# Loads of the head spread over three issuers, query in 1 KB runs, and the combined matrix M built through VectorE turns of w2

## The chip, the core and the metric

One core of a Trainium2 chip runs the whole program. The metric is the device time of one execution in microseconds. TensorE is called PE, VectorE DVE, ScalarE ACT, GpSimd POOL, SyncE SP; PEld is PE's load of stationary operands, and SPq is SP issuing DMAs.

## What is computed

Three layers follow each other: an attention through 32 memory slots (4 batches, 8 heads, 576 positions, width 64), a mixture of 4 experts with all experts weighted (2304 rows, width 512, inner width 1024), and a soft mixture of 8 experts with 4 slots each.

```
a = softmax(phi, over 32 slots);  k_m = a.T @ k;  v_m = a.T @ v          # per batch and head
x = softmax(q @ k_m.T / 8) @ v_m                                         # 2304 x 512
out1 = sum_e p[:, e] * (relu(x @ w1[e]) @ w2[e])                         # 4 experts, p normalised
logits = out1 @ phi2                                                     # 2304 x 32
d = softmax(logits, over rows);  c = softmax(logits, over slots)
slot_in = d.T @ out1;  slot_out[e] = relu(slot_in[e] @ v1[e]) @ v2[e]
out = c @ slot_out
```

## The kernel before

The product of w2 is never applied to rows one by one. For the logits the kernel builds M = w2[e] @ phi2 in eight chunks (an expert's half of 512 inner rows each, `m_chunk`), and for `slot_in` it sums the hidden rows first and applies w2 at the end. So the main part is: for each batch b, for each of eight chunks n, a product G of v_m and w1 (`g_mult`, L676), then `up`: four column blocks of 128 times two ranges of 288 rows, six matmuls each (L751 to L753) between the attention weights A and G. ACT puts the relu into one of six buffers (L759), DVE turns it (L765), POOL multiplies by p (L769). After each chunk `logits` (L787) multiplies the relu's buffers by M; a buffer is free once both have read it. At a unit's end a `group` (L957) takes the sums. After the last unit come w2, v1, v2 and the combination, streamed in blocks of 1 MB (L1191 to L1402).

The head is the attention of batch 0. `memory`: phi is loaded, its maxima taken (L438 to L456), the exponential made on ACT (L477), k_m and v_m summed on PE (L495, L500, L514, L518), scaled and turned (L530, L538, L542). `query`: a tile of 128 positions is turned on PE by four 128x128 transposes (L584), copied by ACT (L588), multiplied with k_m (L596), turned on DVE (L610), its maxima taken (L611), the difference on POOL (L613), the exponential on ACT (L616), the sum and its inverse on DVE (L620 to L622), the product on POOL (L624), a turn on DVE (L630), and then written as a rounded part on ACT (L636) and a rest on POOL (L638), which together are A. The first `up` needs the first three of the five tiles.

An M chunk before: one DMA of 1 MB brings 512 rows of w2 as 8 KB runs; sixteen 128x128 transposes on PE (L818) go through two banks and are copied out by DVE (L824) and ACT (L828) in turn; four matmuls with phi2 (L835) follow, a copy on ACT (L841), four small matmuls that fold the four parts (L847), and a DVE copy into M (L852).

Order: every piece of work is added to a `Plan` with an engine, a cost and a due time `at`; the plan's own sum of costs then sorts it, and each engine runs its list strictly in that order. DMAs are all issued by SP, in order. At most eight of them are under way, since eight semaphores are used in turn and an issue waits for the DMA eight before it. `uses(...)` chooses among buffers and banks from due times.

## Time and profile before

| | us |
|---|---|
| median of 3 runs (lowest, highest) | 522.94 (522.83, 523.92) |
| the profiled execution | 522.95 |
| its span, first to last instruction | 521.2 |
| PE busy in the span | 488.3 |
| DVE, ACT, POOL busy | 301.2, 203.6, 211.4 |

The span is 1.75 us shorter than the time of the same execution; a change of the span is carried over to the time one to one. The chain of waits follows the work back from the last instruction: 86% of it is PE.

### The profile page before, as it was taken

Reading aid. Unit: us, or ns where it says so; the run is one execution under the profiler, and the core shown is the slowest. Engines: PE = TensorE matmul, PEld = TensorE weight load, DVE = VectorE, ACT = ScalarE, POOL = GpSimd, SP = SyncE. Lnnn points to the kernel's source line nnn. Section 1 sums busy time; section 2 is a strip of 40 time slices with the busy share of each in tenths; the row PEclk is TensorE's granted clock in tenths of the full one; section 3 lists DMA queues with packets and bytes.
Section 4 is the critical chain, followed back from the end, with each engine's and each line's share of the span. In section 5 each row is a group of like instructions: output and inputs, shape, how many; then the busy total and the mean of one; then the engine's idle time right before and its main releaser. Section 6 shows DMA issues by size and latency. Waiting matters only on the chain.

```text
span 521.2 us, 13391 instructions
## 1 busy us (share of the span) xinstructions
PE 488.3 (94%) x5668; PEld 342.9 (66%) x5668; DVE 301.2 (58%) x605; ACT 203.6 (39%) x479; POOL 211.4 (41%) x252
## 2 busy tenths in 40 slices
PE   4899999999999999999999999999999989998583
PEld 2677787877876887787678877756687855332141
DVE  6488554668685758778684776756577544010022
ACT  2354444545541545555154555514442420010032
POOL 0244412547641548764144776524654840000000
PEclk9999999999999999999999999999999999899586
DMA  7999757333521853352082444524246987999967
GB/s 222 215 352 314 301 170 228 117 108 91 178 81 47 282 166 112 102 170 95 16 285 103 138 163 140 187 81 161 87 153 239 325 329 303 423 421 423 367 196 251
DMA packets 71835, 106.08 MB, mean 204 GB/s; under 512 B 28768, under 2 KB 49760, under 8 KB 66144
## 3 DMA queue, kind: packets, MB, share of 16 engines
q1 hardware_dynamic: 71776, 105.23, 60.0%
q8 instruction: 44, 0.72, 0.6%
q14 instruction: 15, 0.12, 0.1%
HBM read 100.50 MB, written 4.72 MB: 202 GB/s over the span
## 4 chain that ended last, share of the span: by engine, by line
PE 86%; DVE 4%; DMA 3%; SPq 3%; ACT 2%; issue 1%; ACTq 0%; DVEq 0%
PE ps L751 15%; PE ps L753 13%; PE ps L752 13%; PE ps L957 8%; PE ps L676 6%; PE ps L787 5%; PE ps L1260 4%; PE ps L818 3%; SPq L349 3%; PE ps L1299 2%; PE ps L794 2%; PE ps L584 2%; PE ps L596 2%; DMA h<-in_moe_w_dram 2%; PE ps L835 1%; DMA h<-in_q_dram 1%
## 5 line engine op out<-in xcount | busy, mean ns | idle before, releaser
L769 POOL TENSOR_TENSOR h<-h,pe 128x576 f32<-128x576 f32 (+1 forms) x160 | 157.2, 992 | 169.3 <-DVE h L765 132.7
L759 ACT ACTIVATE hts<-ps 128x288 f32<-128x288 f32 x256 | 105.6, 413 | 155.7 <-PE ps L753 154.3
L751 PE MATMUL ps<-A,g 128*128 128x288 f32 x512 | 161.8, 316 | 0.2 <-ACT g L685 0.2
L753 PE MATMUL ps<-A,g 128*128 128x288 f32 x512 | 151.3, 295 | 0.2 <-DVE g L687 0.2
L752 PE MATMUL ps<-A,g 128*128 128x288 f32 x512 | 151.0, 295 | 0.0
L765 DVE STREAM_TRANSPOSE h<-hts 128x576 f32<-128x576 f32 (+1 forms) x160 | 102.5, 649 | 52.7 <-ACT hts L759 52.2
L751 PEld LDWEIGHTS ps<-A,g 128*128 128x128 f32 x512 | 96.1, 188 | 38.0 <-issue 26.9
L753 PEld LDWEIGHTS ps<-A,g 128*128 128x128 f32 x512 | 96.1, 188 | 0.8 <-DVE g L687 0.8
L752 PEld LDWEIGHTS ps<-A,g 128*128 128x128 f32 x512 | 96.3, 188 | 0.2 <-POOL A L638 0.2
L687 DVE TENSOR_TENSOR g<-ps,g 128x512 fp32r<-128x512 f32 x64 | 40.9, 680 | 19.2 <-ACT g L685 19.2
L685 ACT CAST g<-ps 128x512 fp32r<-128x512 f32 x64 | 34.5, 589 | 20.0 <-PE ps L676 20.0
L957 PE MATMUL ps<-h,dts 32*32 32x512 f32 x1152 | 40.0, 597 | 1.6 <-DVE dts L939 1.6
L676 PE MATMUL ps<-raw,vb 64*32 64x512 f32 x512 | 35.5, 601 | 0.4 <-DVE g L687 0.4
L957 PEld LDWEIGHTS ps<-h,dts 32*32 32x32 f32 x1152 | 22.8, 103 | 15.2 <-issue 4.7
L787 PE MATMUL ps<-hts,M 128*32 128x288 f32 x384 | 28.3, 412 | 0.0
L613 POOL TENSOR_TENSOR atts<-atts,small 128x256 f32<-128x256 f32 (+1 forms) x20 | 11.5, 574 | 25.7 <-DVE small L611 25.6
L1349 DVE COPY v<-ps 128x512 f32<-128x512 f32 x4 | 2.6, 686 | 29.4 <-PE ps L1341 29.4
L818 PE MATMUL ps<-ident,h 128*128 128x128 f32 x128 | 18.5, 276 | 0.3 <-DVE g L687 0.3
L824 DVE COPY h<-ps 128x512 f32<-128x512 f32 x16 | 11.1, 691 | 10.6 <-PE ps L818 10.5
L787 PEld LDWEIGHTS ps<-hts,M 128*32 128x32 f32 x384 | 10.0, 109 | 10.0 <-issue 4.5
L818 PEld LDWEIGHTS ps<-ident,h 128*128 128x128 f32 x128 | 14.9, 143 | 1.4 <-DVE g L687 0.5
L638 POOL TENSOR_TENSOR A<-atts,A 128x256 fp32r<-128x256 f32 (+1 forms) x20 | 13.6, 681 | 5.4 <-ACT A L636 5.2
(176 smaller groups left out, 530.7 us busy)
## 6 DMA issues: line engine op xcount, KB each, us to landing
raw<-in_moe_w_dram SPq DMA_DIRECT2D x32, 1024.0 KB, 5.2
v<-in_moe_w_dram SPq DMA_DIRECT2D x20, 1024.0 KB, 10.0
h<-in_moe_w_dram SPq DMA_DIRECT2D x18, 1024.0 KB, 8.3
h<-in_k_dram SPq DMA_DIRECT2D x8, 512.0 KB, 5.3
h<-in_v_dram SPq DMA_DIRECT2D x8, 512.0 KB, 6.8
atts<-in_moe_w_dram SPq DMA_DIRECT2D x4, 1024.0 KB, 7.6
atts<-in_q_dram SPq DMA_DIRECT2D x12, 256.0 KB, 5.7
atts<-in_phi_dram SPq DMA_DIRECT2D x8, 256.0 KB, 3.6
```

Of the source, the lines that this page charges most:

```text
L676: nc.tensor.matmul(bank[bs[c]][32 * i:32 * i + 32, :], vb[b % 2][64 * c:64 * c + 64, 32 * i:32 * i + 32], t()[64 * c:64 * c + 64, i, :], s ...
L685: add(ACT, act(512), lambda c=c, src=src: nc.scalar.copy(out=placed(g()[:, 2 * c]), in_=src), r=[pk(bs[c])], w=[wk(o + 1024 * c, 512)], at ...
L687: add(DVE, dve(512), lambda c=c, src=src: nc.vector.tensor_tensor(out=placed(g()[:, 2 * c + 1]), in0=src, in1=placed(g()[:, 2 * c].bitcast ...
L751: nc.tensor.matmul(t, gh, ah, start=(c == 0), stop=False)
L752: nc.tensor.matmul(t, gh, al, start=False, stop=False)
L753: nc.tensor.matmul(t, gl, ah, start=False, stop=(c == 1))
L759: add(ACT, act(w), lambda: nc.scalar.activation(out=t[:, o0 - base:o1 - base], in_=bank[bm][:, 0:w], func=ACTF.Relu,), r=[pk(bm)], w=[wk(h ...
L765: add(DVE, dve(width), lambda: nc.vector.transpose(out=h_of(u, e)[:, kx], in_=t), r=[wk(ho, width)], w=[hk], at=at + 0.4)
L769: add(POOL, pool(width), lambda: nc.gpsimd.tensor_tensor(out=h_of(u, e)[:, kx], in0=h_of(u, e)[:, kx], in1=share, op=ALU.mult), r=["pe"], ...
L787: nc.tensor.matmul(lb[r0:r0 + 32, 0:HB], M[:, 4 * n + a, :], at_place(hos[a] + o0, o1 - o0), start=(first and h == 0), stop=(not first and ...
L818: nc.tensor.transpose(bank[bk][:, 128 * c:128 * c + 128], wn()[:, a, 128 * c:128 * c + 128], ident)
L957: nc.tensor.matmul(bank[S0 + p][32 * c:32 * c + 32, :], dtv[rows, tb, :], h_pair(u, ep)[rows, :, :, tb, :], start=(tb < 2), stop=(tb >= nt ...
```

## The change

The query tile 4 and the small tables go out from POOL's queue, half of phi and of k from ACT's, and the rest stays with SP. Query of batch 0 comes as four DMAs by pairs of heads, each run 1 KB (four positions of one head) where it was four DMAs of one position in four with 256-byte runs. Its turn on PE is now a true matmul against the identity with one head of 64 columns as the stationary operand, eight per tile; all four tiles need all four DMAs. The q block is placed before v in the SP queue. An exponential of one column on ACT stands ahead of the real ones. An M chunk is four DMAs of 32 partitions with 1 KB runs, four DVE transposes of 32x32 blocks (SBUF to SBUF), 32 matmuls of 64 rows by 32 columns with 128 moving columns, and one DVE transpose into M. The normalising of p is due later, M's due times are wider apart, and batch 1's loads are due 4 units later. Loads inside `dma` are reckoned by their run length.

```
     def load_q_all(at):
         o = R[2]
-        t = at_place(o, 2048).rearrange("p (r h d) -> p r h d", h=8, r=4)
+        t = at_place(o, 2048).rearrange("p (h r d) -> p h r d", h=8, r=4)
+        for j in range(4):
+            hs = slice(2 * j, 2 * j + 2)
+            dma(
+                t[:, hs], q[0, hs, 0:512, :].rearrange("h (p r) d -> p h r d", r=4), 262144,
+                w=[wk(o + 512 * j, 512)], at=at,
+            )
         for ti in range(4):
-            dma(
-                t[:, ti], q[0, :, 0:512, :].rearrange("h (p r) d -> r p h d", r=4)[ti], 262144,
...
+            q_of[0, ti] = ([t[:, h, ti, :] for h in range(8)], [wk(o + 512 * j, 512) for j in range(4)])
...
         def flip():
-            for j in range(4):
-                nc.tensor.transpose(t[:, j, 0:n], js[j][0:n], ident[0:n, 0:n])
...
+            m = 128 * 4 // len(js)
+            for x in range(len(js)):
+                j, y = divmod(m * x, 128)
+                if m == 128:
+                    nc.tensor.transpose(t[:, j, 0:n], js[x][0:n], ident[0:n, 0:n])
+                else:
+                    nc.tensor.matmul(
+                        t[y:y + m, j, 0:n], js[x][0:n], ident[0:n, 0:n], start=True, stop=True
+                    )
...
     def m_chunk(n, ats):
...
+        for p in range(4):
+            fh, dh = divmod(p, 2)
+            src = w2[e, FH * f:FH * f + FH, 256 * dh:256 * dh + 256]
+            src = src.rearrange("(h x k) d -> h x k d", h=2, k=8)[fh]
...
         for a in range(4):
-            bk = g_bank()
...
+            add(DVE, dve(512), lambda a=a: nc.vector.transpose(
+                out=at_place(o + 2048 + 512 * a, 512), in_=wn(a, 1)),
...
+        def part():
+            for c in range(8):
+                for q in range(4):
+                    rows = slice(64 * (q // 2), 64 * (q // 2) + 64)
+                    nc.tensor.matmul(
+                        bank[bk][32 * q:32 * q + 32, 0:128], phi_of()[rows, c, :], wt()[rows, q % 2, c],
+                        start=(c == 0), stop=(c == 7),
                     )
...
-    load_phi(0, -190)
-    load_kv(0, 0, -189)
-    load_kv(0, 1, -188)
-    load_q_all(-187)
+    load_phi(0, -190, (SP, ACT))
+    load_kv(0, 0, -189, (SP, ACT), (SP, ACT))
+    add(ACT, 1.4, lambda: nc.scalar.activation(out=ind[:, 3:4], in_=ind[:, 2:3], func=ACTF.Exp), r=["cst"],
+        w=["ind"], at=-188.9)
+    load_q_all(-188.5)
+    load_kv(0, 1, -188, (SP, SP), (POOL, POOL))
     load_w1(0, -186)
-    load_q(0, 4, -185)
...
-    m_at = [2.5, 6.2, 10.5, 14.5, 18.5, 22.5, 26.5, 30.5]
+    m_at = [3, 8, 13, 18, 25, 29, 36, 43]
```

On PE in the head, at the turns of batch 0's query tiles (L584 before, L587 and L589 now; L596 or L603 is the product with k_m), before:

```order
L584 MATMUL ps_95<-ident,h_91 128x128 x4
L538 MATMUL ps_94<-ident,atts 128x128
L584 MATMUL ps_96<-ident,h_91 128x128 x4
L596 MATMUL ps_99<-atts,kb_78 32x128 x8
L584 MATMUL ps_100<-ident,h_91 128x128 x4
L596 MATMUL ps_94<-atts,kb_78 32x128 x8
```

and now:

```order
L538 MATMUL ps_93<-ident,atts 128x128
L587 MATMUL ps_97<-ident,atts 128x64 x4
L589 MATMUL ps_94<-ident,h_90 64x128 x8
L589 MATMUL ps_95<-ident,h_90 64x128 x8
L589 MATMUL ps_99<-ident,h_90 64x128 x8
L589 MATMUL ps_100<-ident,h_90 64x128 x8
L603 MATMUL ps_98<-atts,kb_77 32x128 x8
```

The first product with k_m stood behind two turned tiles and stands now behind all five; the turn of k_m (L538) has moved ahead of the first tile.

On DVE, from the turn of the last query tile to the first piece of M (L824 or L829 is w2, L852 or L845 the write of M, L765 or L772 the turn of the relu, L438 the maxima of batch 1), before:

```order
L824 COPY h_105<-ps_99 128x4x128
L765 STREAM_TRANSPOSE h_91<-hts 128x576
L1122 COPY pe<-ps_100 128x4x4x4
L1126 COPY pe<-ps_100 128x2x4
L765 STREAM_TRANSPOSE h_91<-hts 128x576
L1122 COPY pe<-ps_101 128x4x4x4
L1126 COPY pe<-ps_101 128x2x4
L1132 COPY pe_76<-pe 64x144 x2
L438 TENSOR_REDUCE atts<-atts 128x128
L852 COPY M<-ps_99 128x128
```

and now:

```order
L1137 COPY pe_75<-pe 64x144 x2
L829 STREAM_TRANSPOSE h_150<-h_150 128x512
L772 STREAM_TRANSPOSE h_90<-hts 128x576
L829 STREAM_TRANSPOSE h_150<-h_150 128x512
L438 TENSOR_REDUCE atts<-atts 128x128
L772 STREAM_TRANSPOSE h_90<-hts 128x576
L438 TENSOR_REDUCE atts<-atts 128x128
L845 STREAM_TRANSPOSE M<-ps_97 128x128
```

Between the tables of p and the write of M's first chunk there are now two turns of w2's second chunk and one more turn of the relu.

## Rows read from the trace of the kernel before

**Rows 1.** The page's first part: busy us (share of the span) xinstructions

```profile
PE 488.3 (94%) x5668; PEld 342.9 (66%) x5668; DVE 301.2 (58%) x605; ACT 203.6 (39%) x479; POOL 211.4 (41%) x252
```

**Rows 2.** What PE waited for, whole span: us in total, times, longest

```profile
PE ps L495 <- ACT atts L477: 1.7, 2, 1.4
...
PE ps L584 <- DMA h<-in_q_dram: 1.3, 1, 1.3
```

**Rows 3.** Chain of waits, the head: start us, us, what

```profile
8.22 7.35 DMA h<-in_q_dram
...
20.00 1.03 PE ps L596 x16
...
30.69 0.13 PE ps L751
```

**Rows 4.** Timeline of the head: start us, us, engine, line, operation, names, forms

```profile
9.66 1.08 PE L495 MATMUL ps<-h,atts 128*32 128x64 f32 x32 [1.44 <-ACT atts L477]
...
14.72 0.48 DVE L530 TENSOR_SCALAR atts<-ps,small 128x64 f32<-128x64 f32 x2
...
17.85 1.10 PE L596 MATMUL ps<-atts,kb 128*32 128x128 f32 x16
...
19.05 0.45 DVE L610 STREAM_TRANSPOSE atts<-ps 128x256 f32<-128x256 f32 x1 [1.46 <-PE ps L596]
...
23.49 0.66 PE L596 MATMUL ps<-h,kb 128*32 128x128 f32 x16
...
24.34 0.46 PE L584 MATMUL ps<-ident,atts 64*128 64x64 f32 x4
```

**Rows 5.** Engines by stage, columns as named in the first line

```profile
core 0: us, PE busy (x) PEld busy (x) DVE busy (x) ACT busy (x) POOL busy (x), PEclk, DMA share, GB/s
22.87:30.69 7.82, 7.38 (x138) 3.89 (x127) 7.44 (x23) 4.50 (x13) 5.16 (x8) 1.00 0.84 306
30.69:50.00 19.31, 19.30 (x150) 15.35 (x150) 16.16 (x38) 9.18 (x22) 7.33 (x10) 1.00 1.09 299
...
70.00:110.00 40.00, 39.86 (x480) 31.80 (x473) 22.94 (x46) 18.29 (x41) 14.10 (x16) 1.00 0.48 151
```

**Rows 6.** Chain of waits from 30.69 to 110, by line

```profile
by line: PE ps L818 19.1%; PE ps L751 14.9%; PE ps L752 12.7%; PE ps L753 12.2%; PE ps L835 9.6%; PE ps L847 9.1%; PE ps L787 5.6%; PE ps L676 3.8%; PE ps L1115 1.8%; DVE g L687 1.6%; ACT ct L841 1.5%; PE ps L596 1.5%; PE ps L495 1.5%; PE p
```

**Rows 7.** Chain of waits around chunk 7 of M, and G's product

```profile
102.80 0.87 PE ps L818 x8
...
106.45 0.99 PE ps L835 x8
...
108.44 0.92 PE ps L847 x8
...
110.67 1.02 PE ps L676 x16
```

**Rows 8.** DVE's groups, 20 to 130: busy us, mean ns | idle before

```profile
L765 DVE STREAM_TRANSPOSE h<-hts 128x576 f32<-128x576 f32 x25 | 19.2, 771 | 9.0 <-ACT hts L759 9.0
L824 DVE COPY h<-ps 128x512 f32<-128x512 f32 x16 | 11.1, 691 | 10.6 <-PE ps L818 10.5
...
L438 DVE TENSOR_REDUCE atts<-atts 128x128 f32<-128x512 f32 x4 | 4.2, 1063 | 1.1 <-DMA atts<-in_phi_dram 1.1
```

**Rows 9.** Chain of waits, whole span: narrow matmuls, four and sixteen abreast

```profile
71.26 0.58 PE ps L495 x32
...
156.23 9.68 PE ps L957 x266
```

**Rows 10.** DMA issues: KB each, us to landing

```profile
h<-in_moe_w_dram SPq DMA_DIRECT2D x18, 1024.0 KB, 8.3
...
h<-in_q_dram SPq DMA_DIRECT2D x4, 256.0 KB, 7.4
```

**Rows 11.** Chain of waits, the end of the program

```profile
479.50 6.91 SPq L349
486.45 9.40 DMA h<-in_moe_w_dram
```

More of the change, by code (lines that the diff above doesn't have):

```diff
@@ L346, in program, with dma @@
     small_at.o = 0
-    def dma(to, of, size, r=(), w=(), at=0.0, cost=0.6):
-        add(SP, cost, lambda: nc.sync.dma_start(
+    def dma(to, of, size, r=(), w=(), at=0.0, run=1024, eng=SP):
+        start = {SP: nc.sync, ACT: nc.scalar, POOL: nc.gpsimd}[eng].dma_start
+        add(eng, 1.0 if eng == POOL else 0.6, lambda: start(
             out=to() if callable(to) else to, in_=of() if callable(of) else of,
-        ), r=r, w=w, at=at, size=size)
+        ), r=r, w=w, at=at, size=0.9 * size * max(1, 1024 // run))
     ph = at_place(PH, 1152).rearrange("p (i m) -> p i m", m=NM)
@@ L383, in load_kv @@
                 kt[64 * c:64 * c + 64, w], src[c, :, 512:576, :].rearrange("i p d -> p i d"),
-                65536, w=[("kt", w, c)], at=at,
+                65536, r=r, w=[("kt", w, c)], at=at + 0.02, run=256, eng=rest[c],
             )
@@ L400, in load_q @@
                 t, q[b, :, 0:512, :].rearrange("h (p r) d -> r p h d", r=4)[ti], 262144,
[L401 removed]
+                w=[wk(o, 512)], at=at, run=256,
             )
@@ L405, in load_q @@
                 t[0:64], q[b, :, 512:576, :].rearrange("h s d -> s h d"), 131072,
-                w=[wk(o, 512)], at=at,
+                w=[wk(o, 512)], at=at, run=256, eng=eng,
             )
         q_of[b, ti] = (
-            [t[:, 2 * j:2 * j + 2, :].rearrange("p c d -> p (c d)") for j in range(4)], wk(o, 512)
+            [t[:, 2 * j:2 * j + 2, :].rearrange("p c d -> p (c d)") for j in range(4)], [wk(o, 512)]
         )
@@ L804, in m_chunk, with wn @@
         e, f = divmod(n, F // FH)
[L805 to L808 removed]
+        o = R[3] if n in (0, 2, 4) else R[4]
+        def wn(q, w):
+            return at_place(o + 512 * q, 512 * w)
         def wt():
[L811 to L830 removed]
@@ L831, in m_chunk @@
+        for a in range(4):
+            add(DVE, dve(512), lambda a=a: nc.vector.transpose(
+                out=at_place(o + 2048 + 512 * a, 512), in_=wn(a, 1)),
+                r=[wk(o + 512 * a, 512)] + [("wn", o, p) for p in range(4)],
+                w=[wk(o + 2048 + 512 * a, 512)], at=ats[1 + a])
         bk = g_bank()
         def part():
-            for c in range(4):
-                nc.tensor.matmul(
-                    bank[bk][32 * c:32 * c + 32, :], phi2_sb[:, c, :], wt()[:, c], start=True, stop=True,
-                )
@@ L838, in m_chunk @@
-        wtk = wk(o + 2048, 2048)
-        add(PE, 0.9, part, r=[("wt", n % 2, a) for a in range(4)] + [wtk, "phi2"], w=[pk(bk)], at=ats[5])
-        mp = ct[:, 0:512]
-        add(ACT, act(512), lambda: nc.scalar.copy(out=mp, in_=bank[bk]), r=[pk(bk)], w=["mp"],
-            at=ats[5] + 0.1)
-        b2 = g_bank()
-        def fold():
-            for a in range(4):
-                nc.tensor.matmul(
-                    bank[b2][:, 32 * a:32 * a + 32], mp[:, 128 * a:128 * a + 128], si,
-                    start=True, stop=True,
-                )
@@ L851, in m_chunk @@
-        add(PE, 0.95, fold, r=["mp", "cst"], w=[pk(b2)], at=ats[6])
-        add(DVE, 0.3, lambda: nc.vector.tensor_copy(
-            out=M[:, 4 * n:4 * n + 4], in_=bank[b2][:, 0:128].rearrange("p (a s) -> p a s", a=4),
-        ), r=[pk(b2)], w=[("M", n)], at=ats[6] + 0.1)
+            for c in range(8):
[4 more added lines that the diff above has]
+                        start=(c == 0), stop=(c == 7),
+                    )
@@ L857, in program @@
+        add(PE, 1.5, part, r=[wk(o + 2048, 2048), wk(R[4] + 4096, 256)] + [("phi2", p) for p in range(4)],
+            w=[pk(bk)], at=ats[5])
+        add(DVE, 0.3, lambda: nc.vector.transpose(
+            out=M[:, 4 * n:4 * n + 4].rearrange("p a s -> p (a s)"), in_=bank[bk][:, 0:128],
+        ), r=[pk(bk)], w=[("M", n)], at=ats[5] + 0.1)
     begun = [False]
@@ L1091, in program @@
         dp[:, 0:16, :].rearrange("p (b r) e -> p b (r e)", b=B),
-        dpv[:, 0:512, :].rearrange("b (p r) e -> p b (r e)", r=4), 32768, w=[("dp", 4)], at=-183,
-    )
-    for b in range(B):
-        p0 = 64 * (b % 2)
-        dma(dp[p0:p0 + 64, 16 + b // 2, :], dpv[b, 512:576, :], 1024, w=[("dp", b)], at=-183)
+        dpv[:, 0:512, :].rearrange("b (p r) e -> p b (r e)", r=4), 32768, run=64, eng=POOL,
+        w=[("dp", 2)], at=-183,
+    )
+    for h in range(2):
+        dma(
+            dp[64 * h:64 * h + 64, 16:18, :], dpv.rearrange("(b h) s e -> h s b e", h=2)[h, 512:576], 2048, run=64,
+            eng=POOL, w=[("dp", h)], at=-183,
+        )
     load_w1(1, -182)
@@ L1111, in norm @@
         )
-    add(DVE, 1.0, norm, r=[("dp", n) for n in range(5)], w=["dpn"], at=2)
+    add(DVE, 1.0, norm, r=[("dp", n) for n in range(3)], w=["dpn"], at=4)
     def spread(x, bk):
```

84 lines of the change are left out of this document (36 added, 48 removed).

## The prediction, made before the changed kernel ran

> **What bounds the kernel now.** I read the page's first part first: PE is busy 94% of the span, DVE 58%, the others about 40% [rows 1]. Then the list of PE's waits: in the head there is one of 1.3 us for query and one of 1.4 for the exponential [rows 2]. The stages say where that leaves slack: from 30.69 to 50, PE is busy 19.30 of 19.31 us and DVE 16.16, and from 70 to 110 PE 39.86 of 40 while DVE has 17 us to spare [rows 5]. So from 30.69 on, whatever leaves PE's list shortens the program, as long as DVE keeps up in the first 20 us. Before 30.69 it is different: there the chain goes through query's landing, PE's turns, and then through the softmax of the tiles on DVE, which is busy 7.44 of the last 7.82 us [rows 3, 5]. The end waits for transfers, on SP and then for w2's landing [rows 11], but those loads start when PE frees their buffers; if PE is earlier by some amount, they are too, and I carry a gain through one to one.
>
> **M on PE, before.** In the chain from 30.69 to 110 (79.3 us) the transposes L818 hold 19.1%, the product L835 9.6%, the fold L847 9.1% and the copy L841, for which PE waited, 1.5% [rows 6]: 39.3%, 31.2 us for eight chunks, or 3.9 each. The pieces of one chunk agree: 8 transposes 0.87 (so 16 take 1.74 or a little more), then 0.99 and 0.92 [rows 7].
>
> **M on PE, now.** One run of 32 products of 64 rows by 32 columns, each 128 columns long. No row has this shape. A product in this number format is two instructions, so a chunk is 64, four of them on different column groups. Nearest in width: 32 instructions of 64 columns, four abreast, take 0.58 us, 16 of 128 columns 0.66 [rows 4, 9]. With twice the columns and twice the count of the first, 64 take 0.58 x 4 = 2.32, less the start counted four times; from the second, 4 x 0.66 = 2.64, again with four starts. Both have the same number of columns in all, and part of each is the start; if that is about 0.16, 0.42 to 0.50 are left, and 4 x 0.42 to 4 x 0.50 with one start is 1.8 to 2.2; the sixteen-abreast run L957 needs 36 ns an instruction (9.68 / 266), and at that pace 64 need 2.3 [rows 9]. I take 2.0, bounds 1.8 and 2.3. Eight chunks: 16.0. **PE saves 31.2 - 16.0 = 15.2 us**, bounds 12.8 and 16.8.
>
> Here a rule weighs against the change. G's product writes its two halves of rows to two banks and takes 1.02 us for sixteen [rows 7]; the new product lets both halves of rows write one bank, on different partitions, and no row has that. The Trainium skill, TensorEngine Tiling (Array Packing), Gotcha 1: PSUM Pressure, says that different row tiles cannot access the same PSUM bank simultaneously. By my reading the outputs lie in different column groups and so do not meet; by the rule they would have to take turns, and the sum would lose what the rival below says.
>
> **DVE's new work for M.** Sixteen copies by DVE at 0.691 go (the other sixteen were ACT's), thirty-two turns come. A turn of 576 columns takes 0.771 [rows 8]; for 512 that is 0.69 by length. After 50 us that is harmless (DVE is free 17 us of 40 [rows 5]). In the first 20 us it is not: as the order shows, both first chunks' eight turns stand ahead of the first write of M and of batch 1's second maximum (1.063 each [rows 8]), where four copies stood. DVE's list there grows by 8 x 0.69 - 4 x 0.69 = 2.8, from 16.2 to 19.0, while PE's shrinks by 2 x (3.9 - 2.0) = 3.8, from 19.3 to 15.5 [rows 5]. PE then waits for DVE at batch 1's maxima and at G, up to 3.4 us. The normalising of p has moved out of this stage into the head, where DVE is idle, and neighbouring DVE operations overlap a little, so I take **2.5 us lost**, bounds 0.5 and 5.
>
> **The head.** Query landed at 15.57 and was the last thing waited for [rows 3]. It is now issued as soon as phi has landed, in runs four times as long, and half of phi and k go out on ACT beside SP; I expect it before 14. But that is hidden: k_m is scaled at 14.72 to 15.20 [rows 4], and in PE's list its turn and everything behind it wait for that. The start of that chain is the softmax of phi, up to 9.66 [rows 4], and it begins with phi's landing, which is the first DMA in either kernel. The early exponential only loads the table, and ACT waited for DVE there anyway: zero, and nothing if that cover goes, because the loads ahead of it are four short issues. POOL's issues are over long before its first subtraction, which waits for a tile of scores.
>
> What costs is the turn of the query tiles. Four transposes become eight products of 64 columns, sixteen instructions; and the first product with k_m now stands behind all of them. In this stretch sixteen instructions of 128 columns, four abreast, took 1.10 us at 17.85 and 0.66 at 23.49 [rows 4]; the clock column says 1.00 in both, but the durations are those of the lower and of the higher of two levels, so I go by the durations. Two abreast stream twice as long: about 1.7 per tile at the lower level and 0.9 at the higher. From 15.20: the turn of k_m to 15.65, tile five (0.46 at the higher [rows 4], 0.8 at the lower) to 16.4, then four tiles, of which some 2.9 run at the lower level until 21.3 (a product at 20.00 still took 1.03 [rows 3]) and 1.1 at the higher: 22.3. The first product ends at 23.0, and DVE starts on the first tile there, not at 19.05 [rows 4]. From there DVE has the work that it did from 22.87 to 30.69 (7.8 us [rows 5]) plus the first two turns and maxima, 0.45 and nearly as much each, 1.8 in all: 9.6, to 32.6. ACT's and POOL's parts bring the first `up` to 33.1 to 33.3 against 30.69 [rows 3]: **2.6 us lost**. Bounds: 0.8 if the clock rises as soon as the turns begin, 4 if they all run at the lower level.
>
> **The rest.** w2 arrives in 1 KB runs, 262 KB a DMA, eight DMAs ahead of the chunk's use; a 1 MB block of before took 8.3 us to land [rows 10], and each chunk has that time between the last turn that frees its place and its own first turn (some 20 us for chunks 2 and 3). Zero, unless the rate falls to a third. Batch 1's loads are due later but their results are needed only at about 147.
>
> **Sum.** -15.2 + 2.5 + 2.6 = -10.1. The span 521.2 becomes 511.1; the execution was 522.95, 1.75 above its span, and equals the median 522.94, so **512.8 us**. The terms' own bounds give 507 to 519.
>
> **Rivals.** (a) The two halves of rows must take turns in their bank. Then each half of a step, two abreast, streams 0.21 us (half of the 0.42 that sixteen need four abreast) and its end is awaited, about as long as the start of 0.16 that I took above [rows 4, 9]. Sixteen such halves a chunk: 6.0 instead of 2.0, eight chunks 32 us; PE no longer waits for DVE, which gives back 2.5: 512.8 + 32 - 2.5 = 542, **slower**. If only the streaming is shared and no end is awaited, a chunk takes 3.6, and 512.8 + 12.8 - 2.5 = 523, no change. It decides from 3.3 us a chunk on. For it speaks that every product of before with two halves of rows uses two banks (`g_mult` gives each half a bank of its own); against it that different column groups end in different partitions. (b) The turns or the loads are slow. If the 64-column products run one after another, not in pairs, the head loses another 3.4 to 5; if w2's DMAs of 32 partitions fill only a quarter of the memory's ports at a time, a chunk lands in some 10 us instead of 3, DVE's list stands still at chunk 3's first turn, and PE runs out of relu buffers for 5 to 8 us. Either gives about 519. For the second speaks the Trainium skill, DMA: Bandwidth & Descriptors, Rules for kernel authors, which asks for 128 partitions and 1 MiB a DMA; no row shows a load to 32 partitions. (c) The head gains what it is meant to: the clock rises with the first products, query's tiles are done by 20, and DVE has slack: 15.2 - 0.8 - 0.5 = 13.9, **507** with the middle price of M, and 505 with the lower. That the change does not do what it says cannot be: the lists show all of it.
>
> **Chances.** Forecast 0.58 (507 to 519), (a) 0.09 for 542 and 0.06 for 523, (b) 0.17, (c) 0.10. The range leaves out 542, half of 523 and the lower half of (c), 0.17 in all: 506 to 524. This kernel's times can be told apart from about 0.2%, so faster means under 521.9: forecast, (c) and most of (b), 0.81; the same, up to 524.0, 0.08; slower 0.11.
>
> **What would show it.** M: the new product's share of the chain, 16 us in eight pieces of 2.0; pieces of 3.6 or 6 are rival (a). Head: the first `up` at about 33, DVE's first tile at 23, query landed before PE's turns wait for it; a first `up` before 31 is (c). DVE: PE waits of one to three microseconds for DVE between 45 and 60, and none later; waits of DVE for w2's DMA are (b). Wrong altogether would be an end that does not move with PE: loads at the end that do not start earlier.

## The result and the profile after

The changed kernel takes **529.63 us** (median of 4 runs, 527.79 to 531.0) against 522.89 beside it: 1.0126 of the time before, 95% interval 1.0103 to 1.0148. It is 1.3% slower, where 512.8 was forecast. The profiled execution took 531.0, the longest of the four; its span is 529.2, 8.0 longer than before. Runs that stood more than 1.5% above the fastest of the same kernel are left out of every median and ratio in this document.

Three marks split these 8.0 us. The first `up` (L758) stood at 39.75, against 30.44 before (the chain of waits names it from 30.69 on [rows 3], where the product ahead of it ends): the head lost 9.3. The first sums of unit 0 (L950) came 121.26 us after it, against 125.72: this stretch gained 4.5. From there to the first v1 product of the end (L1268) both kernels need 292.1. From that product to the end of the span it took 76.1 us, against 72.9: the end lost 3.2. The sum is 9.3 - 4.5 + 3.2 = 8.0.

PE's waits up to 165 us, after the change (us in total, times, longest):

```profile
PE ps L445 <- DMA atts<-in_phi_dram: 7.2, 1, 7.2
PE ps L1120 <- issue: 3.3, 1, 3.3
PE ps L839 <- DVE g L694: 2.6, 1, 2.6
PE ps L495 <- DMA h<-in_k_dram: 2.4, 1, 2.4
PE ps L449 <- DVE atts L438: 1.1, 1, 1.1
```

Neither the wait for query nor the one for the exponential [rows 2] is there any more. In their place PE waits for k, and it stops for 3.3 us with nothing to wait for that the profile shows. The chain of waits in the head tells where the time goes:

```profile
2.04 10.20 DMA h<-in_k_dram
12.38 1.08 PE ps L495 x32
...
18.45 0.62 PE ps L587 x4
19.07 6.03 PE ps L589 x64
25.10 1.05 PE ps L603 x32
...
31.69 3.33 issue
35.02 0.27 PE ps L1120
35.30 1.05 PE ps L1051 x4
36.34 2.00 PE ps L683 x16
...
38.80 0.59 ACT g L692
```

The sums with k begin at 12.38 instead of 9.66 [rows 4]; the 64 instructions that turn query's first four tiles take 6.03 us; then comes the stop, and behind it the product for G takes 2.00 instead of 1.02 [rows 7]: it runs at the lower of the clock's two levels (1.2 and 2.4 GHz). Two ten-microsecond stages, with the columns of [rows 5], show the granted clock of 0.71 and 0.78 that follows:

```profile
30.00:40.00 10.00, 6.39 (x57) 3.20 (x49) 7.24 (x20) 4.09 (x11) 4.69 (x9) 0.71 1.14 233
40.00:50.00 10.00, 9.80 (x104) 8.99 (x105) 7.15 (x17) 2.87 (x9) 2.04 (x4) 0.78 0.74 217
```

The stretch from the first `up` to unit 0's sums as one row each, first of before, then of after:

```profile
30.44:156.16 125.72, 124.97 (x1272) 98.29 (x1271) 84.15 (x160) 62.41 (x144) 58.03 (x62) 1.00 0.59 186
```

```profile
39.75:161.01 121.26, 117.09 (x1521) 93.60 (x1521) 89.91 (x168) 48.18 (x118) 57.20 (x60) 0.97 0.67 174
```

PE is busy 7.9 us less. The granted clock was at the lower level until 44.4 and again from 64.9 to 68.3, 8 us of this stretch in all, which cost about half of that, 4.0; so PE's work shrank by some 11.9. Of that, 4.0 went to the clock and 3.4 to idle time (4.17 us against 0.75). The gain is there; 7.4 of it are given back.

### The profile page after: what moved, and what is told of

Same layout as the page of the kernel before. It is cut to its first block, busy times and chain, and to the rows that moved or that the text cites. A ratio compares the mean times of both kernels' runs of the same rounds, so it can differ in the third digit from the quotient of the medians.

```text
span 529.2 us, 14023 instructions
## 1 busy us (share of the span) xinstructions
PE 486.4 (92%) x5972; PEld 344.0 (65%) x5972; DVE 309.5 (58%) x621; ACT 190.5 (36%) x456; POOL 217.2 (41%) x262
## 4 chain that ended last, share of the span: by engine, by line
PE 86%; DVE 5%; DMA 4%; SPq 1%; ACT 1%; issue 1%; POOL 0%; ACTq 0%; DVEq 0%
PE ps L758 15%; PE ps L760 12%; PE ps L759 12%; PE ps L950 8%; PE ps L683 6%; PE ps L794 5%; PE ps L1268 4%; PE ps L839 4%; PE ps L1307 2%; PE ps L801 2%; PE ps L603 2%; DMA h<-in_k_dram 2%; PE ps L495 2%; DMA h<-in_moe_w_dram 2%; SPq L350 1%; PE ps L587 1%
## 5 line engine op out<-in xcount | busy, mean ns | idle before, releaser
L758 PE MATMUL ps<-A,g 128*128 128x288 f32 x512 | 161.9, 316 | 0.4 <-ACT A L643 0.3
L772 DVE STREAM_TRANSPOSE h<-hts 128x576 f32<-128x576 f32 (+1 forms) x160 | 102.4, 648 | 53.5 <-ACT hts L766 52.9
L758 PEld LDWEIGHTS ps<-A,g 128*128 128x128 f32 x512 | 96.9, 189 | 36.5 <-issue 24.8
L694 DVE TENSOR_TENSOR g<-ps,g 128x512 fp32r<-128x512 f32 x64 | 40.9, 678 | 15.1 <-ACT g L692 15.1
L950 PE MATMUL ps<-h,dts 32*32 32x512 f32 x1152 | 40.0, 597 | 1.6 <-DVE dts L932 1.6
L950 PEld LDWEIGHTS ps<-h,dts 32*32 32x32 f32 x1152 | 22.8, 103 | 15.2 <-issue 4.7
L839 PE MATMUL ps<-h 64*32 64x128 f32 x512 | 19.9, 307 | 2.6 <-DVE g L694 2.6
L829 DVE STREAM_TRANSPOSE h<-h 128x512 f32<-128x512 f32 x32 | 20.6, 677 | 0.9 <-DMA h<-in_moe_w_dram 0.8
L839 PEld LDWEIGHTS ps<-h 64*32 64x32 f32 x512 | 16.3, 113 | 6.0 <-DVE g L694 3.5
```

The costliest lines, as they stand in the source:

```text
L694: add(DVE, dve(512), lambda c=c, src=src: nc.vector.tensor_tensor(out=placed(g()[:, 2 * c + 1]), in0=src, in1=placed(g()[:, 2 * c].bitcast ...
L758: nc.tensor.matmul(t, gh, ah, start=(c == 0), stop=False)
L772: add(DVE, dve(width), lambda: nc.vector.transpose(out=h_of(u, e)[:, kx], in_=t), r=[wk(ho, width)], w=[hk], at=at + 0.4)
L839: nc.tensor.matmul(bank[bk][32 * q:32 * q + 32, 0:128], phi_of()[rows, c, :], wt()[rows, q % 2, c], start=(c == 0), stop=(c == 7),)
L950: nc.tensor.matmul(bank[S0 + p][32 * c:32 * c + 32, :], dtv[rows, tb, :], h_pair(u, ep)[rows, :, :, tb, :], start=(tb < 2), stop=(tb >= nt ...
```

## The experiments

First `up`, first sums of unit 0 (S) and span are of the profiled execution, in us; the ratio is to runs of the kernel before made beside it on the same chip, with its 95% interval (medians of before were 522.9 to 524.2). From S to the first v1 product all kernels need 292.1 to 292.6.

| kernel | median | ratio | first `up` | S | span |
|---|---|---|---|---|---|
| before | 522.89 | 1 | 30.44 | 156.16 | 521.2 |
| changed | 529.63 | 1.0126 (1.0103-1.0148) | 39.75 | 161.01 | 529.2 |
| m_only | 524.74 | 1.0025 (1.0007-1.0044) | 34.77 | 157.99 | 523.2 |
| head_only | 533.49 | 1.0200 (1.0179-1.0222) | 36.49 | 163.11 | 531.2 |
| all_sp | 521.93 | 0.9991 (0.9964-1.0018) | 33.01 | 153.05 | 520.3 |
| old_query | 524.13 | 1.0033 (0.9995-1.0071) | 30.34 | 153.35 | 520.5 |
| no_pool | 526.27 | 1.0052 (1.0037-1.0067) | 33.82 | 156.85 | 524.1 |
| end_order | 527.43 | 1.0071 (1.0045-1.0098) | 38.61 | 158.62 | 525.6 |
| w2_held | 539.99 | 1.0293 (1.0251-1.0336) | 34.56 | 171.80 | 539.0 |
| more_pe | 528.24 (one run) | - | 40.12 | 158.80 | 526.5 |
| m_later | 521.15 | 0.9965 (0.9945-0.9986) | 29.82 | 152.95 | 518.8 |
| m_held | 521.52 | 0.9943 (0.9921-0.9965) | 32.73 | 155.03 | 521.0 |
| w2_half | 519.01 | 0.9916 (0.9882-0.9950) | 29.76 | 150.08 | 515.0 |
| turns_half | 528.22 | 1.0104 (1.0075-1.0133) | 30.43 | 160.35 | 526.3 |
| m_sized | 522.59 | 0.9968 (0.9950-0.9986) | 30.16 | 152.84 | 519.3 |
| m_sized_held | **517.81** | **0.9894 (0.9863-0.9925)** | 29.96 | 148.81 | 514.6 |

### The two halves of the change apart

m_only puts the new `m_chunk`, its due times, phi2's four loads (on SP) and the later loads of batch 1 into the kernel before; head_only puts the old ones into the changed kernel. Of m_only's diff, the due times:

```diff
-    m_at = [2.5, 6.2, 10.5, 14.5, 18.5, 22.5, 26.5, 30.5]
+    m_at = [3, 8, 13, 18, 25, 29, 36, 43]
+    m_was = [None, None, 0, 1, 2, 3, 5, 6]
...
```

> The kernel before with the new M alone (w2 in 1 KB runs, VectorE turns, two products in row halves, the later loads of batch 1); the head, its queues and its query tiles stay as before. Theory: the two halves of the change pull in opposite directions, and the whole loss sits in the head; from the first `up` to the first sums of unit 0 the changed kernel was already 5.0 us shorter than before, and here the first `up` starts at 30.7 again as in [rows 3]. So 514 to 519 us, faster by 0.8 to 1.7 %. Rival: the gain of 5.0 us behind a late head came only from VectorE and the transfers having had 9.8 us more to run ahead, and with the early head the VectorE turns stop TensorE longer; then 521 to 525 us, no gain.

> The changed kernel with the old M (one load of w2, PE transposes, fold) and the new head. Theory: the loss is in the head, so the first `up` comes at 38 to 41 us against 30.7, and the time is 531 to 536 us (522.9 + 8 to 10, and up to 3 at the end). Rival: the late first `up` needs the new M's loads and turns beside it; then the first `up` comes at 33 or earlier and the time is 523 to 526 us.

head_only's time came as the theory had it; its first `up`, at 36.49, came earlier than expected, with k's sums at 10.55 and without the stop of 3.3 us. m_only did not come out so: it gained nothing. Its head shows one reason: TensorE waited 4.3 us for the second w1 block, which SP had issued behind phi2's new loads in runs of 128 B. From the first `up` to S it took 123.2 us: a gain of 2.5 only, half of what the changed kernel has there. So the head's loss and M's gain don't simply add (533.49 + 524.74 - 522.9 would be 535): a late head gives w2 time to land.

### The queues

all_sp issues every load of the head on SP; no_pool changes only those that GpSimd issued, v's tails among them. The last query tile, phi2 and dprob are treated as v's tails are in this diff of all_sp against the changed kernel:

```diff
-    load_phi(0, -190, (SP, ACT))
-    load_kv(0, 0, -189, (SP, ACT), (SP, ACT))
+    load_phi(0, -190)
+    load_kv(0, 0, -189)
-    load_kv(0, 1, -188, (SP, SP), (POOL, POOL))
+    load_kv(0, 1, -188)
...
```

> The changed kernel with every load of the head on SyncE's queue again (phi, k, v tails, last query tile, phi2, dprob); the query in 1 KB runs, the turns and the new M stay. Theory: packets of three queues share the 16 engines, and the small ones slow k's: on one queue the second k half lands at 9.5 to 10.5 us instead of 12.2 and phi's tail at 5.3 instead of 7.2; the first `up` comes 2 to 3 us earlier and the time is 526 to 528 us. Rival: k is late because the query's loads are issued behind it and share the engines with it, whatever the queue; then k's sums still start at 12 or later and the time stays at 529 to 531 us.

> The changed kernel with GpSimd's loads (v's tails, the last query tile, dprob, phi2) on SyncE's queue, ScalarE's halves of phi and k kept. Theory: GpSimd's packets of 2 to 4 KB are what slows phi's tail and k; without them phi's tail lands at 5.2 to 5.6 and k's sums start at 9.6 to 10.2 instead of 12.4, and the time is 524 to 528 us. Rival: two hardware queues side by side are enough to slow k; then k's sums start at 11 or later.

On one queue the sums with k begin at 9.65, just as before the change, and TensorE's wait for phi ends at 5.2 instead of 7.2; the time fell by more than forecast, to that of the kernel before. With GpSimd's loads alone taken off they begin at 10.18, and the wait for phi ends at 5.9. In the six profiles with all three queues k's sums began at anything from 10.2 to 12.4; in the nine of the table with all loads on one queue, between 9.5 and 9.7. So one profile at 10.18 doesn't part GpSimd's share from ScalarE's by itself, but the packets do. Between 8 and 13 us (before, after and no_pool; the rows that begin with q are a queue, its packets, MB and share of the 16 engines):

```profile
DMA packets 2058, 1.62 MB, mean 324 GB/s; under 512 B 611, under 2 KB 2058, under 8 KB 2058
...
q1 hardware_dynamic: 2058, 1.62, 112.2%
```

```profile
DMA packets 1550, 1.10 MB, mean 220 GB/s; under 512 B 704, under 2 KB 1473, under 8 KB 1550
...
q1 hardware_dynamic: 1044, 0.82, 84.7%
q0 software_dynamic: 216, 0.19, 19.3%
q10 hardware_dynamic: 290, 0.09, 11.9%
```

```profile
DMA packets 1856, 1.65 MB, mean 330 GB/s; under 512 B 297, under 2 KB 1856, under 8 KB 1856
```

The engines were busy throughout in all three, but with GpSimd's queue (q0) among them a packet of 1 KB took 80 ns on average instead of 54, and a third less was moved. Without GpSimd's loads it took 54 again and 330 GB/s were moved, although ScalarE's queue (q10) had been as busy as SP's just before (49.4% and 46.5% of the engines from 4 to 8 us); with everything on SP (all_sp) it is 53 ns and 332 GB/s. So it is GpSimd's loads beside the others that slow phi and k, and not the spreading as such. Whether that comes from their queue or from their form wasn't tried. ScalarE's halves cost 0.5 us at k in this profile; no_pool's span stays 3.9 us above that of all_sp, 0.8 of it up to the first `up` and 3.0 from there to S, and the cause of those 3.0 stays open.

### The query tiles

old_query, against the changed kernel, in `load_q_all` (the views for four transposes a tile follow from it):

```diff
-        for j in range(4):
-            hs = slice(2 * j, 2 * j + 2)
-            dma(t[:, hs], q[0, hs, 0:512, :].rearrange("h (p r) d -> p h r d", r=4), 262144, ...)
+        for ti in range(4):
+            dma(t[:, ti], q[0, :, 0:512, :].rearrange("h (p r) d -> r p h d", r=4)[ti], 262144, ...)
```

> The changed kernel with the query of the head loaded as before (runs of 256 B, one DMA for a tile) and turned by four transposes for a tile instead of eight products of 64 columns; queues and M stay changed. Theory: 64 turns at the lower clock level (94 ns each) take 6.0 us where 16 transposes take about 2, and the first scores stand behind all of them; so VectorE's first tile comes at 21 to 23 us instead of 25.8, the first `up` 3 to 4 us earlier, the time 525 to 527 us. Rival: what follows is held by something else (the stop of 3.3 us of TensorE in the middle of the table's products, the order of ScalarE's copies), and the 3 to 4 us turn into waiting; then the first `up` is still at 39 or later and the time 528 to 531 us.

VectorE's first tile came at 19.24, even earlier than expected, and the first `up` at 30.34, at its old place. The rival's wait did not take over. Not all of the 9.4 us are the query's: in this profile k's sums began at 10.16 instead of 12.38, and the stop of 3.3 us and the lower clock behind it are not there. The price of the turns with k in time is read from all_sp: its 48 + 16 instructions took 4.88 and 1.02 us, and its first tile came at 21.13, 2.1 later than before. The times of old_query lie between 521.0 and 528.6; the profiled one (522.34) is one of the shorter, and what lengthens the others was not seen.

### The stop of 3.3 us

The page of the changed kernel has a queue of instruction packets (number, MB, share):

```profile
q8 instruction: 47, 0.77, 0.6%
```

These are 47 packets of 16 KB. TensorE's recorded instructions are 11993 (5972 products, 5972 weight loads and 49 semaphore instructions), 255 for each packet; in the kernel before they are 11395 for 44, 259 each. So TensorE is fed in blocks of some 256 instructions, 128 pairs of weight load and product. Counted in these instructions, the first fetch of the kernel before begins when 194 have been issued, so that the second is due at the 450th; it begins 0.5 us after that one. In the changed kernel the 450th was issued at 26.3, but the fetch began at 31.98. At 31.5 the 705th had been issued, two whole blocks behind the place of the first fetch: what had been fetched was used up. Two runs try that.

w2_held changes the loads in `m_chunk` and their due time, more_pe adds one line ahead of the other calls of `warm`:

```diff
+                r=[("vb", 0)] if n < 2 else (),
...
-        m_chunk(n, [n - 181.5 if n < 2 else m_at[m_was[n]] + 1.6, m0, m0 + 0.5, m0 + 1, m0 + 1.5, m0 + 2.4])
+        m_chunk(n, [0.01 * n - 166 if n < 2 else m_at[m_was[n]] + 1.6, m0, m0 + 0.5, m0 + 1, m0 + 1.5, m0 + 2.4])
```

```diff
+    warm(12, [pk(LB)], -177.5)
```

> The changed kernel with the eight loads of w2's first two chunks held back until v_m is turned (about 28 us); nothing else moves in the head. Theory: the stop of 3.3 us in the middle of the table's product is TensorE out of instructions. It used 256 between the end of the first block of instructions and 31.4 us; the next block's fetch, due at 26.2, began at 31.98, behind w2's packets. With w2 held the fetch begins within 1 us of its due time as in the kernel before (0.5 us), TensorE doesn't stop, the first `up` comes at 35 to 36.5 instead of 39.75, and the time is 524 to 527 us (the two chunks' turns come later, which may cost 1 to 2). Rival: the stop belongs to the product or to its data; then it stays, the first `up` is at 39 or later, and the time 529 to 532.

> The changed kernel with 24 more products of the identity on TensorE while it waits for phi (48 instruction pairs more at the head of its list; their results are read by nobody). Theory: TensorE stops where its fetched instructions end, that is after as many pairs as in the changed kernel (358 from its start), now 48 pairs earlier in the program: a pause of 1 to 4 us in or before the first product for G (L683) or the fourth tile's scores (L603), and none in the table's product L1120. Rival: the pause belongs to L1120 or its data; it stays there, at pair 406.

The added products are one pair each, 24 and not the 48 that the text says. The stop came after the 705th instruction again, and so earlier in the program: the 16 pairs of the last tile's scores, the 6 of L1051 and the first of the table's product lie between, and it now stands ahead of those scores and not in the table's product. The chain of more_pe:

```profile
27.17 0.59 PE ps L603 x16
27.77 1.02 PE ps L683 x16
28.79 4.09 issue
32.88 0.68 PE ps L603 x16
```

The run end_order (below), with the changed kernel's head, stopped after the 705th too, for 3.3 us, and there the fetch began at 31.2. In the other kernels of the table the second fetch began between the 472nd and the 649th instruction, and none stopped at the 705th. One of them, m_sized (below), stops twice later on, in the middle of a run of like products, after the 1729th and the 1985th: four and five whole blocks of 256 behind the 705th.

```profile
74.70 0.30 PE L495 MATMUL ps<-h,atts 128*32 128x64 f32 x2 [0.77 <-issue]
...
82.64 0.31 PE L500 MATMUL ps<-atts 64*32 64x64 f32 x6 [1.06 <-issue]
```

That TensorE ran out of instructions is thus shown. Where the fetch stood meanwhile is less sure: all engines of the DMA were busy (share 1.14 from 30 to 40), and with w2 held back it began at 27.4, still 3.2 late but in time, so that TensorE didn't stop and the first `up` came at 34.56, a little earlier than expected. The time, 540, was a plain miss: M's first product then comes at 57.1 instead of 47.2, VectorE's list stands at turns of w2 (14.4 us of waits for it), and S comes 137 us after the first `up`.

The Trainium skill, Runtime: NRT & Kernel Launch, Instruction fetch mechanics, says that instructions come in blocks of 16 KiB, 256 each, fetched while the block before is executed, and calls the fetch mostly hidden. The size agrees with the 47 packets here; hidden it was not in these four profiles.

### The end

end_order changes one line of `dma`. On TensorE this moves one item: eight products L1307, which stood ahead of the first half's L1405 and L1349, stand behind these and ahead of the second half's L1405.

```diff
-        ), r=r, w=w, at=at, size=0.9 * size * max(1, 1024 // run))
+        ), r=r, w=w, at=at, size=(1.0 if at >= 193 else 0.9) * size * max(1, 1024 // run))
```

> The changed kernel with the planner's old size of a transfer for the loads of the end (due from 193 on); its order differs from the changed kernel's in one place alone: the last eight products L1307 of the second half of the output stand behind the first half's output products again, as before the change. Theory: in the changed kernel the whole output waits for the last w2 block, and that is what its end is longer by; from the first v1 product to the end of the span it took 76.1 us against 72.9 before, and here it takes 73 again, so 526 to 528 us. Rival: the end is longer only because the clock was lower there; then it stays at 75 to 76 and the time at 529 to 531.

The chain at the second half of the output, first of the changed kernel, then of end_order:

```profile
510.92 1.25 PE ps L1372 x8
512.17 2.02 PE ps L1405 x4
...
514.64 2.08 PE ps L1349 x14
...
517.49 2.08 PE ps L1349 x11
```

```profile
509.20 0.99 PE ps L1307 x16
510.19 1.21 PE ps L1405 x4
...
511.84 1.14 PE ps L1349 x15
...
513.75 1.14 PE ps L1349 x10
```

With the eight products between the halves, the second half's fold and output products take 1.21 and 2 x 1.14 us; without them, 2.02 and 2 x 2.08. From the first product behind the last block's landing to the last copy it is 18.9 us in the kernel before, 19.2 in end_order, 22.0 in the changed kernel and 22.1 in all_sp, which has the changed order. So neither text was quite right: the order costs about 3 us, and it costs them through the clock, not through waiting. Of these, 1.2 showed in this span's end (74.9 us from the first v1 product); from its last copy to the end of the span it took 1.9 longer than before the change.

### What M gives back

m_later is m_only with phi2's loads due later. Each of the next four differs from m_later by the lines that follow in its turn; m_sized_held has those of m_held and of m_sized.

```diff
-            32768, w=[("phi2", p)] + ([wk(R[4] + 4096, 256)] if p == 0 else []), at=-184,
+            32768, w=[("phi2", p)] + ([wk(R[4] + 4096, 256)] if p == 0 else []), at=-181.8,
```

> The kernel before with the new M alone, as in the run m_only, but phi2's four loads in runs of 128 B are issued behind the second w1 block instead of ahead of it. Theory: in m_only TensorE waited 4.3 us for that w1 block, and the first `up` came at 34.8 instead of 30.7; here it comes at 30.5 to 31.5, and with m_only's 123.2 us from there to unit 0's first sums the time is 520 to 522 us, a gain of 0.2 to 0.6 %. Rival: the new M as such gives nothing, since what PE saves on it comes back as waits for VectorE and lower clock behind each wait; then an earlier start only lets the waits grow, and the time stays at 523 to 525.

m_later's first `up` starts at 29.82 and its time is as the theory had it, 0.35% below that before, but the stretch to S still takes 123.1 us. VectorE's timeline there, and what waited from 30 to 153 us:

```profile
52.77 0.32 DVE L837 STREAM_TRANSPOSE M<-ps 128x128 f32<-128x128 f32 x1 [1.36 <-PE ps L831]
59.86 0.71 DVE L821 STREAM_TRANSPOSE h<-h 128x512 f32<-128x512 f32 x1 [6.77 <-DMA h<-in_moe_w_dram]
60.50 0.73 DVE L765 STREAM_TRANSPOSE h<-hts 128x576 f32<-128x576 f32 x1
```

```profile
DVE h L821 <- DMA h<-in_moe_w_dram: 7.9, 2, 6.8
...
PE ps L751 <- ACT hts L759: 4.9, 1, 4.9
```

The third chunk's first turn waits 6.8 us for w2, the turn of h (L765) stands behind it, ScalarE finds no free relu buffer, and PE stops for 4.9. That is the prediction's rival (b), its second half, with a stop at the low end of its 5 to 8 us. In the changed kernel VectorE waited for w2 only 0.8 us in all: the late head hid it.

m_held:

```diff
-        load_kv(b, 1, base + 10 + late, r=[("M", 2)] if late else ())
+        load_kv(b, 1, base + 12 + late, r=[("M", 2)] if late else ())
...
-            load_q(b, ti, at + 18)
+            load_q(b, ti, at + 18, r=[("M", 2)] if late else ())
```

> The run m_later (the kernel before, the new M alone, phi2 behind the second w1 block) with batch 1's v and its query tiles held until M's third chunk is written; in m_later they were issued ahead of w2's third and fourth chunk. Theory: in m_later VectorE stood 6.8 us before the third chunk's first turn because w2 had not landed; ScalarE's relu then found no free buffer, TensorE stopped 4.9 us and ran 3.4 us at the lower clock. Here w2 lands in time, TensorE's idle time from the first `up` to unit 0's first sums falls from 6.5 us to 3 or less, and the time is 514 to 517 us, 1.2 to 1.7 % faster than before. Rival: the transfers are at their limit from 30 to 75 us whatever the order, so that what is held back now delays the next (w1, k of batch 1), and the time stays at 519 to 522.

w2_half (the loads) and turns_half (the turns):

```diff
-        for p in range(4):
+        for p in range(4 if n < 2 else 2):
```

```diff
-        for a in range(4):
+        for a in range(4 if n < 2 else 2):
```

> The run m_later with two of the four transfers of w2 left out for M's chunks 2 to 7 (what they would bring is taken from an earlier chunk, so M differs; every instruction of the engines stays). This leaves out 3.1 of the 8.4 MB of w2. Theory: the new M's saving on TensorE is given back by transfers, which take w2 in runs of 1 KB to 32 partitions at some 86 ns a KB against 44 in runs of 8 KB; then VectorE's wait of 6.8 us for w2 and TensorE's idle 6.5 us nearly vanish and the time is 514 to 517 us. Rival: VectorE's own work takes the gain; then the time stays at 519.5 to 522.

> The run m_later with two of the four VectorE turns of w2 left out for M's chunks 2 to 7 (what they would write is taken from an earlier chunk, so M differs), 12 turns of 0.68 us, 8.2 us of VectorE; the transfers stay. Theory (transfers): TensorE still waits for w2 through VectorE, and the time is 519.5 to 521.5 us. Rival (VectorE's work): the time falls by 4 us or more, to 517 or below.

Taking away 3.1 MB of w2 gained 2.1 us on m_later (the two intervals just meet), less than expected: one wait of 4.6 us for w2's third chunk is left. Taking away 8.2 us of VectorE's work lost 7: the planner, with a shorter list, puts the turns earlier, and VectorE waits 15.1 us for w2. Neither run leaves the rest alone: both change the order of VectorE's list too, and turns_half came out as neither of its texts had it. That VectorE's list stands still for w2 in m_later is shown; how much its own work would take if w2 were in time, these two don't show. Holding back batch 1's v and query alone (m_held) gave m_later's time, as its rival had it; its VectorE waited 4.5 instead of 7.9 us for w2, but PE now waited for batch 1's k (3.8); in this profile query also landed late (a wait of 4.4), which is why its first `up` stands at 32.73.

m_sized:

```diff
-                262144, w=[("wn", o, p)] + ([wk(o, 2048)] if p == 0 else []), at=ats[0] + 0.001 * p,
+                2 * 262144, w=[("wn", o, p)] + ([wk(o, 2048)] if p == 0 else []), at=ats[0] + 0.001 * p,
```

> The run m_later with w2's transfers given to the planner at twice their size, about what a KB of theirs took (86 ns against 44). Nothing is left out; only the order changes: on VectorE the turns of h, the subtraction of the maxima and their sums now stand ahead of the third chunk's turns. Theory: m_later loses to VectorE's list standing still at a turn whose w2 has not landed, with work for TensorE behind it; here that work goes first, TensorE's idle time from the first `up` to unit 0's sums falls from 6.5 us to 3 or less, and the time is 514 to 518 us. Rival: the transfers as such hold M up; TensorE then waits for M or for the products of w2 instead, and the time stays at 519.5 to 522.

> m_sized with batch 1's v and query tiles held until M's third chunk is written. Theory: with VectorE's list no longer blocked, what is held back costs or gives little, within 1.5 us of m_sized. Rival: w2's third chunk is still what is waited for, and this is 2 to 4 us faster than m_sized.

Each of the two on m_later gave nothing that can be told apart; both together gave 3.3 us. m_sized's theory missed: no wait of VectorE for w2 is left there, but PE still idles 6.42 us up to S, 2.2 of them for VectorE's turns of w2, 1.8 for ScalarE's copies of query tiles and 1.8 in the two stops for instructions shown above. m_sized_held gained what its rival said or a little more, 4 to 5 us on m_sized, but not for its reason, since w2 was not what m_sized waited for. In m_sized_held VectorE waits for w2 once, 1.6 us, the clock is never lowered from the first `up` to S, and PE idles 3.45 us:

```profile
29.96:148.81 118.85, 115.40 (x1527) 91.73 (x1527) 89.84 (x173) 48.75 (x120) 57.03 (x61) 1.00 0.86 202
```

This version, the old head with the new M, phi2 behind w1, batch 1's transfers held and w2 sized for the planner as it lands, is 1.1% faster than the kernel before and faster than the changed one by some 12 us.

Two more runs load w2 to 64 partitions at a time, m_wide2 otherwise like m_later and m_wide2_held like m_held:

```diff
-        for p in range(4):
-            fh, dh = divmod(p, 2)
-            src = w2[e, FH * f:FH * f + FH, 256 * dh:256 * dh + 256]
-            src = src.rearrange("(h x k) d -> h x k d", h=2, k=8)[fh]
+        for fh in range(2):
+            src = w2[e, FH * f + 256 * fh:FH * f + 256 * fh + 256, :]
+            src = src.rearrange("(x k) (y d) -> y x k d", k=8, y=2)
...
```

> The run m_later with each chunk of w2 loaded by two transfers of 512 KB to 64 partitions in place of four of 256 KB to 32; runs of 1 KB, places and sums are the same. Theory: the new M gives back on the transfers what it saves on TensorE: between 30 and 80 us the packets of 1 KB took 77 ns each in m_later (w2's some 86) against 56 in the kernel before, and the 16 engines were busy throughout; that is so because a transfer to 32 partitions is slow, and to 64 it takes some 60 to 70 ns a packet, w2's third chunk lands earlier, and the time is 515 to 519 us. Rival: runs of 1 KB of w2 cost that much whatever the partitions; then the packets stay at 75 to 80 ns and the time at 520 to 522.

> m_wide2 with batch 1's v and query tiles held until M's third chunk is written (as in m_held). Theory (the transfers are the limit between 30 and 80 us): the order matters little, and the time is within 1 us of m_wide2's. Rival (the order ahead of the third chunk decides): 2 to 4 us below m_wide2.

Both failed, at 683 and 679 us. The question of 32 or 64 partitions stays open, as does that of the order: here something else rules. SP's issues in m_wide2_held:

```profile
25.86 32.14 SPq L349 DMA_DIRECT2D h<-in_moe_w_dram x4
```

Four issues took 32 us, 8 each, and the share of the 16 engines in that time was 0.16. The source pattern had its dimension of two outermost; that this left most engines without work is likely but wasn't tried.

## Why the prediction was wrong

**M on PE: 15.2 forecast, 11.8 measured.** The product's eight pieces in the chain are seven of 2.29 and one of 3.33, which ran at the lower clock level, 19.4 us against 31.2 [rows 6]. The mechanism was right; the price 2.0 was too low, and 2.29 is the bound that came from the narrow run L957 [rows 9]. At 2.29 for all eight it would be 12.9, just inside the bounds of this term.

```profile
47.19 2.29 PE ps L839 x64
...
65.61 3.33 PE ps L839 x64
...
127.16 2.29 PE ps L839 x64
```

Rival (a) is false. The Trainium skill, TensorEngine Tiling (Array Packing), Gotcha 1: PSUM Pressure, says that row tiles cannot access one bank simultaneously; by that a chunk would have taken 3.6 to 6.0. Two halves of rows wrote one bank on different partitions in 2.29 us.

**VectorE: 2.5 lost, forecast; 7.4 given back in the changed kernel, 7.5 in m_later (idle time and clock together).** The turns cost what was said (677 ns, forecast 0.69). In the changed kernel TensorE's waits for VectorE are also of the kind and the size that were forecast, 1.1 us at 58 and 2.6 at 63, and VectorE waited for w2 hardly at all:

```profile
L829 DVE STREAM_TRANSPOSE h<-h 128x512 f32<-128x512 f32 x32 | 20.6, 677 | 0.9 <-DMA h<-in_moe_w_dram 0.8
```

What had no term there is the clock: 4.0 us, 2.3 of them still behind the head's stop and 1.7 behind the wait of 2.6. With the head in time (m_later) the loss is another one: it begins with w2's landing, which the prediction held at "zero, unless the rate falls to a third". The working treated w2 as 1 MB in 8.3 us, whatever its runs. Between 30 and 80 us packets of 8 KB took 44 ns a KB before; in m_later those of 1 KB took 77, w2's alone by the remainder some 86. Twice as much time of 16 engines that were busy already [rows 5] is no zero: the share of 1.09 in that row could have told it.

**The head: 2.6 lost, forecast; 9.3 lost.** The failing sentence is that the chain begins with phi's landing, "which is the first DMA in either kernel", and so can't move. First is not alone: other queues now send at the same time, and GpSimd's slows the rest. TensorE's wait for phi ended 2.0 later and k's sums began 2.7 later, and so the first tile came at 25.79 instead of 23.0. The turns themselves were priced rightly: from the scaled k_m to the last of the four tiles it is 7.1 us in the forecast (15.20 to 22.3) and in the trace (17.97 to 25.10). Without GpSimd's and ScalarE's queues (all_sp) the first tile comes at 21.13 and the first `up` at 33.0, as forecast, though in part by luck: 48 of the 64 turning instructions run there ahead of k_m's turn, from 14.27, which makes the first tile earlier by 1.9, and the table's product then waits 2.0 us for VectorE's turn of the last tile. The rest is what no row of before showed: the stop for instructions, 3.3, and behind it the clock: 1 us on G's product, and 0.78 granted on average from 40 to 50. Together 2.6 + 2.7 + 3.3 + 1.0 make 9.6, near the 9.3. The early exponential was put at zero, and is: in all_sp PE waits 1.4 us at L495 for ScalarE, as in [rows 2].

**The end: "one to one" was wrong.** The start of the end did move with PE (453.09 - 161.01 = 448.24 - 156.16 = 292.08). But the planner's new size for transfers had moved eight products in TensorE's list, and the working never looked there: 3.2 us, of which the order makes some 3.

Point by point: rival (b)'s second half was there, hidden in the changed kernel by its late head; (c) was not, and its sum is off by 2 (13.9 us less make 509, and 507 with the lower price of M). A time slower than before was forecast by (a) alone, whose mechanism is false; it came from the head and the end, which the terms held at 2.6 and 0.

## What to carry to other kernels

A transfer that keeps its place in the list is not safe when others start on other queues beside it: here GpSimd's loads made each packet of the one that everything waited for half as long again, and ScalarE's did not, so try the queues one by one. Price what is added by the ns a KB of rows with the same runs. A list that is worked through in order stands still at the first item whose data is late, so the cost that the planner takes for a transfer must be the measured one; and read the whole order after a change of such a cost, the end too. A stop of TensorE can be paid twice, once as a wait and once as clock: behind the changed kernel's 2.6 us the clock was at its lower level for 3.4, behind m_sized's 2.2 it was not.

## What the runs showed of the hardware

- TensorE can run out of instructions. It stood still for 3.3 to 4.1 us in three profiles, each time after its 705th recorded instruction, two blocks of 256 behind the first fetch's place, because the next fetch came 5.6 to 6.1 us late while the DMA engines were full; in m_sized it stopped twice more, for 0.8 and 1.1. Narrow products in quick succession use up a block sooner: the turns of query alone are half of one.
- With GpSimd's loads on their own queue beside SP's and ScalarE's, a third less was moved than with one queue (220 against 324 to 332 GB/s from 8 to 13 us), at equal busy share; SP's and ScalarE's side by side moved 330.
- Two halves of rows into one PSUM bank, on different partitions, ran without taking turns that a duration shows: 2.29 us for 64 instructions.
- Loads of w2 in runs of 1 KB to 32 partitions took about twice the engine time of runs of 8 KB (some 86 against 44 ns a KB).
- A transfer of 512 KB whose source has a dimension of two outermost took SP 8 us to issue, and the engines stood idle for most of it.
